# Scores and values of a sigmoid attention in one tile shape, with a routed block behind it

## The chip, the cores and the metric

The kernel runs on one core of a Trainium2 chip. The metric is the device time of one execution in microseconds.

## The reference

```python
# q, k, v: 8 x 12 x 448 x 64 (batch, head, token, width), float32
scores = scale * np.matmul(q, k.transpose(0, 1, 3, 2)) - np.log(S)
attn = 1.0 / (1.0 + np.exp(-scores))
attn_out = np.matmul(attn, v)
x = attn_out.transpose(0, 2, 1, 3).reshape(B, S, H * D)      # 8 x 448 x 768
scores = np.einsum('bsd,d->bs', x, w_gate)
out = x.copy()
for b in range(B):
    top_idx = np.argpartition(-scores[b], capacity)[:capacity]   # 128 of 448 tokens
    xe = x[b, top_idx]
    ye = np.maximum(xe @ w1, 0.0) @ w2                           # 768 -> 1024 -> 768
    g = 1.0 / (1.0 + np.exp(-scores[b, top_idx]))
    out[b, top_idx] = xe + g[:, None] * ye
```

## The kernel before, in words

The heads are taken four at a time (a quad: 32 of the 64 widths of four heads fill 128 partitions, `e` is the half of the width), and two quads make a stage `s`: there are twelve stages, and three quads a batch. `turn` transposes a quad's keys and queries on VectorE in blocks of 32. A stage has seven units (`unit`, L180): a unit makes the scores of 128 keys with 448 queries for four heads, in tiles of 32x128 (32 rows of the array for a head), two passes of `e`; unit 3 takes the last 64 keys of both quads instead, in tiles of 32x64. Its results fill two score tiles `psc` of two banks each, of a pool of three, and ScalarE turns each into a tile `attn` with one sigmoid over 896 columns (L200).

`values` (L204) multiplies attention by values one stage later: for each pair of heads `pr`, full pieces of 128 keys (L213, tile 128x64, two heads side by side) and half pieces of 64 keys (L224, 64x64), accumulated in the banks `oa` and `ob`, one for each quad of the stage. When a bank is complete, `take` (L235) transposes it into `x_b` on VectorE; `gate_part`, `gate` and `store` follow.

The routed block of a batch: `rank` (L268) spreads the gates over all partitions with a matmul by ones (L271), copies them (ScalarE, L274), transposes them, counts for each token how many are above it, in four places of 128 tokens (VectorE, L285 and L288), and makes the selection matrix `sel` (L295). `select` (L298) turns it into row numbers (L303) and gathers the rows `xe`. `turn_rows` (L317) transposes them on TensorE in two halves (L323), each copied to `xeT` by VectorE (L325). `ffn1` (L334; three groups, of 3, 3 and 2 blocks) and `ffn2` (L343; three groups) follow, and a scatter writes the rows.

All order is written out by hand in `stream`: after each unit come the value pieces that PACKED or SPREAD names for it, then short routed steps due there, then one group of the queue `ready` by `go`, mostly in bank `ob`. In the first two stages with values no routed group is ready. DMAs go in program order through SP's queue; `load_v(s)` is issued at the first unit of stage `s`, for use in stage `s + 1`. Every matmul of the program is recorded as two matmul instructions and two weight loads.

Of the kernel before, what the change touches and what calls it, by code (L numbers as in the profile page):

```python
# [9 lines left out]
F32 = mybir.dt.float32  # L10
# [7 lines left out]
def kernel(  # L18
# [48 lines left out]
    rows = ctx.enter_context(tc.tile_pool(name="rows", bufs=2))  # L67
    moe = ctx.enter_context(tc.tile_pool(name="moe", bufs=1))
    ps_sc = ctx.enter_context(tc.tile_pool(name="ps_sc", bufs=3, space=PSUM))
    ps_a = ctx.enter_context(tc.tile_pool(name="ps_a", bufs=1, space=PSUM))  # L70
    ps_b = ctx.enter_context(tc.tile_pool(name="ps_b", bufs=1, space=PSUM))

    def bank(which):
        if which == "psc":
            return ps_sc.tile([P, 2, 512], F32, name="psc")[:, 0]
        return (ps_a if which == "oa" else ps_b).tile([P, 512], F32, name=which)
# [52 lines left out]
    earlier = const.tile([P, NC, S], F32, name="earlier")  # L129
# [50 lines left out]
    def unit(s, n):  # L180

        psc = [ps_sc.tile([P, 2, 512], F32, name="psc") for _ in range(2)]
        if n == NF:
            parts = [(x, slice(HK, TB), x * Dh, Dh) for x in range(2)]
        else:
            x, c = divmod(n, NF + 1)
            parts = [(x, slice(4 * c, 4 * c + 4), 0, P)]
        for e in range(2):
            for x, blk, p0, np_ in parts:
                for h in range(4):  # L190
                    d = slice(h * TT, (h + 1) * TT)
                    nc.tensor.matmul(  # L192
                        psc[h // 2][p0:p0 + np_, h % 2, :S],
                        kT[2 * s + x][d, e, blk, :].rearrange("d r t -> d (r t)"),
                        qT[2 * s + x][d, e].rearrange("d r t -> d (r t)"),
                        start=(e == 0), stop=(e == 1))
        for pr in range(2):
            a = attnp.tile([P, 2, S], F32, name=f"attn{pr}", bufs=(NU + 1, NU + 3)[pr])
# [3 lines left out]
    x_tiles, gate_parts, st = {}, {}, {}  # L202

    def values(s, pr, what):  # L204

        tv, th = raw_v[s]
        if (s, pr) not in outs:
            outs[s, pr] = [bank("oa"), bank("ob")]
        o = outs[s, pr]
        if what[0] == "f":  # L210
            _, x, c = what
            for j in range(2):
                nc.tensor.matmul(  # L213
                    o[x][j * Dh:(j + 1) * Dh, :S],
                    tv[:, 4 * x + 2 * pr + j, c * Dh:(c + 1) * Dh],
                    attn[s, pr, (NF + 1) * x + c][:, j, :],
                    start=(x == 0 and c == 0), stop=(x == 1 and c == NF - 1))
            if (x, c) == (1, NF - 1):
                take(s, pr, 1)
        else:  # L220
            for x in range(2):
                p = slice(x * Dh, (x + 1) * Dh)
                for j in range(2):
                    nc.tensor.matmul(  # L224
                        o[x][j * Dh:(j + 1) * Dh, :S], th[p, 2 * pr + j, :],
                        attn[s, pr, NF][p, j, :], start=(x == 1), stop=(x == 0))
            take(s, pr, 0)

    def take(s, pr, x):

        b, g = divmod(2 * s + x, NG)
        if g == 0 and pr == 0:
            x_tiles[b] = rows.tile([P, TB, HP, TT], F32, name="x_b")
            gate_parts[b] = rows.tile([P, TB, NG], F32, name="gate_p")
        nc.vector.transpose(x_tiles[b][:, :, 2 * g + pr, :],  # L235
                            outs[s, pr][x][:, :S].rearrange("p (r t) -> p r t", t=TT))
# [31 lines left out]
    def rank(b, where="oa"):  # L268
        tg = tok_gate[b % 2]
        ps = bank(where)  # L270
        nc.tensor.matmul(ps[:, :S], ones, st[b].pop("diag").rearrange("p r t -> p (r t)"),  # L271
                         start=True, stop=True)
        rep = moe.tile([P, S], F32, name="rep")
        nc.scalar.activation(rep, ps[:, :S], AF.Copy)  # L274
        rep_t = moe.tile([P, TB, TT], F32, name="scr")
        nc.vector.transpose(rep_t, ps[:, :S].rearrange("p (r t) -> p r t", t=TT))
        for a in range(4):
            p = slice(a * TT, (a + 1) * TT)
            n = len(range(a, TB, 4))
            nc.vector.tensor_copy(tg[p, :n, 1], rep_t[p, a:TB:4, 0])  # L280
        for c in range(NC):
            n = P if c < NC - 1 else LAST
            own = tg[:n, c, 1:2]
            junk = moe.tile([P, S], F32, name="scr")
            nc.vector.tensor_scalar(out=junk[:n], in0=rep[:n], scalar1=own, scalar2=0.0,  # L285
                                    op0=ALU.is_gt, op1=ALU.add, accum_out=above[:n, c:c + 1])
            junk = moe.tile([P, S], F32, name="scr")
            nc.vector.scalar_tensor_tensor(  # L288
                out=junk[:n], in0=rep[:n], scalar=own, in1=earlier[:n, c, :],
                op0=ALU.is_equal, op1=ALU.mult, accum_out=level[:n, c:c + 1])  # L290
        place = moe.tile([P, NC], F32, name="place")
        nc.vector.tensor_add(place, above, level)
        for c in range(NC):
            n = P if c < NC - 1 else LAST
            nc.vector.tensor_scalar(out=sel[:n, c], in0=iota_r[:n], scalar1=place[:n, c:c + 1],  # L295
                                    scalar2=None, op0=ALU.is_equal)

    def select(b, s0, n, where):  # L298

        tg = tok_gate[b % 2]  # L300
        pk = bank(where)
# [15 lines left out]
    def turn_rows(b, n, half, where="oa"):  # L317
        if half == 0:
            st[b]["xeT"] = moe.tile([P, KD, P], F32, name="xeT")
        ps = bank(where).rearrange("p (k n) -> p k n", n=P)  # L320
        for t in range(3):
            tt = half * 3 + t
# [188 lines left out]
```

## Time and profile before

| | |
|---|---|
| median of 3 runs | 545.96 us (541.93 to 546.1) |
| the profiled execution | 545.69 us, span 543.9 us |
| TensorE busy | 500.3 us, 92% of the span |
| VectorE, ScalarE busy | 223.4 us, 177.5 us |
| mean granted TensorE clock | 0.97 |

The span runs from the first to the last recorded instruction; the rows are from this execution. PE is TensorE's matmul, PEld its weight loads, DVE VectorE, ACT ScalarE, POOL GpSimd, SP the engine that issues most DMAs. A record of PE that ends a block is shown until its modelled end, so the step from one block's start to the next one's tells more than its length.

### The profile page before, as it was taken

What the parts mean: (1) busy time and instruction counts of PE and PEld (TensorE: products, weight loads), DVE (VectorE), ACT (ScalarE), POOL (GpSimd) and SP (SyncE); (2) the same over time, 40 slices, a digit from 0 to 9 for tenths busy, and PEclk for the clock granted to TensorE, in tenths of its full rate; (3) what the DMA queues carried; (4) which work ended last, traced back from release to release, by engine and by line L of the source; (5) the groups of instructions that cost most, each with busy time, mean ns of one, the idle gap of its engine ahead of it and who ended that gap; (6) DMA issues with size and microseconds to landing.
All of it is one profiled execution on the core that took longest, in us unless ns stands there. A gap on an engine that the chain in (4) does not pass through costs nothing. (4 is left out here: it accounts for less than half of the span.)

```text
span 543.9 us, 8454 instructions
## 1 busy us (share of the span) xinstructions
PE 500.3 (92%) x3584; PEld 288.2 (53%) x3584; DVE 223.4 (41%) x474; ACT 177.5 (33%) x209; POOL 27.3 (5%) x46
## 2 busy tenths in 40 slices
PE   4999987989999999949999999995899999988995
PEld 2333333355565664526566566444357457558894
DVE  3307284573531482581062067177115216455101
ACT  3845451533332343232342343341334234101010
POOL 8000000000000000000000000000100000000100
PEclk9999997989999999998999999997999999999899
DMA  8694988989135379289124157758802007537200
GB/s 249 174 277 151 250 165 157 287 141 207 32 103 130 56 128 252 48 129 256 33 69 119 48 97 133 208 90 144 231 4 65 30 7 127 100 64 127 71 30 29
DMA packets 203397, 68.28 MB, mean 126 GB/s; under 512 B 182048, under 2 KB 194400, under 8 KB 203360
## 3 DMA queue, kind: packets, MB, share of 16 engines
q1 hardware_dynamic: 201952, 61.36, 52.0%
q0 software_dynamic: 1408, 6.39, 3.7%
q8 instruction: 28, 0.46, 0.4%
q14 instruction: 9, 0.07, 0.0%
HBM read 42.57 MB, written 25.17 MB: 125 GB/s over the span
## 5 line engine op out<-in xcount | busy, mean ns | idle before, releaser
L200 ACT ACTIVATE attn<-psc,bias_s 128x896 f32<-128x896 f32 x168 | 160.2, 1004 | 191.8 <-PE psc L192 185.8
L192 PE MATMUL psc<-qT,kT 32*128 32x448 f32 (+1 forms) x1536 | 157.8, 567 | 9.1 <-DVE qT L178 6.5
L192 PEld LDWEIGHTS psc<-qT,kT 32*128 32x128 f32 (+1 forms) x1536 | 63.7, 174 | 79.1 <-issue 53.6
L334 PE MATMUL ob<-xeT,w_sb 128*128 128x128 f32 x576 | 73.6, 289 | 13.2 <-DVE xeT L325 13.2
L334 PEld LDWEIGHTS ob<-xeT,w_sb 128*128 128x128 f32 x576 | 71.1, 203 | 22.3 <-DVE xeT L325 13.5
L213 PE MATMUL ob<-attn,raw_v 128*64 128x448 f32 x288 | 61.1, 552 | 0.0
L235 DVE STREAM_TRANSPOSE x_b<-oa 128x448 f32<-128x448 f32 x24 | 15.6, 650 | 108.6 <-PE oa L224 108.5
L213 PE MATMUL oa<-attn,raw_v 128*64 128x448 f32 x288 | 59.9, 548 | 0.0
L343 PE MATMUL ob<-w_sb,hT 128*128 128x256 f32 x256 | 58.9, 383 | 0.0
L343 PEld LDWEIGHTS ob<-w_sb,hT 128*128 128x128 f32 x256 | 47.3, 190 | 12.6 <-issue 6.8
L213 PEld LDWEIGHTS ob<-attn,raw_v 128*64 128x64 f32 x288 | 18.1, 137 | 41.3 <-issue 41.3
L213 PEld LDWEIGHTS oa<-attn,raw_v 128*64 128x64 f32 x288 | 18.5, 136 | 37.4 <-issue 35.8
L235 DVE STREAM_TRANSPOSE x_b<-ob 128x448 f32<-128x448 f32 x24 | 15.6, 650 | 50.3 <-PE ob L213 50.3
L175 DVE STREAM_TRANSPOSE kT<-raw_k 128x384 f32<-128x384 f32 x48 | 24.6, 549 | 16.3 <-PE psc L192 11.1
L336 ACT ACTIVATE hT<-ob 128x384 f32<-128x384 f32 (+1 forms) x18 | 8.2, 455 | 69.1 <-PE ob L334 57.0
L343 PE MATMUL psc<-w_sb,hT 128*128 128x256 f32 x128 | 30.2, 396 | 0.0
L343 PEld LDWEIGHTS psc<-w_sb,hT 128*128 128x128 f32 x128 | 25.2, 199 | 4.3 <-issue 0.7
L345 DVE SCALAR_TENSOR_TENSOR xe<-ob,gate,xe 128x256 f32<-128x256 f32 x16 | 7.7, 479 | 46.4 <-PE ob L343 46.4
L248 DVE TENSOR_REDUCE gate_p<-scr 128x14 f32<-128x896 f32 x24 | 26.1, 1087 | 0.8
L334 PE MATMUL psc<-xeT,w_sb 128*128 128x128 f32 x192 | 23.8, 288 | 2.6 <-DVE xeT L325 2.6
L224 PE MATMUL ob<-attn,raw_h 64*64 64x448 f32 x96 | 24.1, 579 | 2.1 <-ACT gate L310 2.1
L242 DVE TENSOR_TENSOR scr<-x_b,wg_b 128x896 f32<-128x896 f32 x24 | 25.7, 1070 | 0.3
(62 smaller groups left out, 257.7 us busy)
## 6 DMA issues: line engine op xcount, KB each, us to landing
raw_k<-in_k_dram SPq DMA_DIRECT2D x24, 448.0 KB
raw_q<-in_q_dram SPq DMA_DIRECT2D x24, 448.0 KB
x_d<-x_b SPq DMA_DIRECT2D x32, 336.0 KB
out_dram<-x_b SPq DMA_DIRECT2D x32, 336.0 KB
raw_v<-in_v_dram SPq DMA_DIRECT2D x48, 192.0 KB
w_sb<-in_moe_w_dram SPq DMA_DIRECT2D x6, 512.0 KB
w_sb<-in_moe_w_dram SPq DMA_DIRECT2D x8, 384.0 KB
raw_h<-in_v_dram SPq DMA_DIRECT2D x48, 32.0 KB
```

The source lines that it names most:

```text
L175: nc.vector.transpose(kT[i][:, e, :HK], sk[:, e, :HK].rearrange("p (m c) d -> p c m d", c=NF))
L192: nc.tensor.matmul(psc[h // 2][p0:p0 + np_, h % 2, :S], kT[2 * s + x][d, e, blk, :].rearrange("d r t -> d (r t)"), qT[2 * s + x][d, e].rea ...
L200: nc.scalar.activation(a, psc[pr][:, :, :S], AF.Sigmoid, bias=bias_s, scale=QK_SCALE)
L213: nc.tensor.matmul(o[x][j * Dh:(j + 1) * Dh, :S], tv[:, 4 * x + 2 * pr + j, c * Dh:(c + 1) * Dh], attn[s, pr, (NF + 1) * x + c][:, j, :], ...
L224: nc.tensor.matmul(o[x][j * Dh:(j + 1) * Dh, :S], th[p, 2 * pr + j, :], attn[s, pr, NF][p, j, :], start=(x == 1), stop=(x == 0))
L235: nc.vector.transpose(x_tiles[b][:, :, 2 * g + pr, :], outs[s, pr][x][:, :S].rearrange("p (r t) -> p r t", t=TT))
L242: nc.vector.tensor_tensor(out=tmp, in0=x_tiles[b][:, :, 2 * g:2 * g + 2, :].rearrange("p r h d -> p r (h d)"), in1=wg_b[:, 2 * g:2 * g + 2 ...
L248: nc.vector.tensor_reduce(out=gate_parts[b][:, :, g], in_=tmp, axis=AX.X, op=ALU.add)
L334: nc.tensor.matmul(ps[:, f - f0, :n], w1_sb[:, t, f * P:(f + 1) * P], xeT[:, t, :n], start=(t == 0), stop=(t == KD - 1))
L336: nc.scalar.activation(st[b]["hT"][:, f0:f1, :n], ps[:, :f1 - f0, :n], AF.Relu)
L343: nc.tensor.matmul(ps[:n, :ND], st[b]["hT"][:, t, :n], w2_sb[:, t, cols], start=(t == 0), stop=(t == KF - 1))
L345: nc.vector.scalar_tensor_tensor(out=xe[:n, cols], in0=ps[:n, :ND], scalar=st[b]["gate"][:n, 0:1], in1=xe[:n, cols], op0=ALU.mult, op1=ALU ...
```

## The change

Scores and values both use tiles of 32x64. A unit is split into two parts of 64 keys, side by side in the array. The values of a stage's four pairs (two quads, two pairs each) are made together in four rounds: in round `n` the row group `r` of the array works for pair `r ^ n`, so that in each round each of the four row groups writes to another bank, and after four rounds each pair has had all four. Round 0 comes after the last unit of the stage, rounds 1 to 3 after the first three units of the next; rounds 0 and 1 also take the 64 keys of unit 3. After each of the first three rounds ScalarE copies one element into a spare column of the bank written last.

The score pool has two tiles instead of three; the four other banks are two tiles `o0` and `o1`, which hold the values of the four pairs from round 0 until they are taken, are lent to the routed block between rounds 3 and 0 (in turn), and to units 1, 3 and 5 of stage 0. `select` uses a score tile. Routed groups stand after units 3, 4 and 5 (two after unit 5). `rank` becomes `spread`, four `rank` of one place each, and `place`, due at two points. `turn_rows` is done at once, with one copy on ScalarE. `earlier` has bytes instead of floats. The value load of the next stage is issued at the first unit of a stage, the second quad's turn after unit 1, the next stage's after unit 5.

The diff is cut to its core; lines that it removes are left out of it, they stand in the kernel above.

```diff
...
+    ps_sc = ctx.enter_context(tc.tile_pool(name="ps_sc", bufs=2, space=PSUM))
+    ps_o = [ctx.enter_context(tc.tile_pool(name=f"ps_o{n}", bufs=1, space=PSUM))
+            for n in range(2)]
+    turns = [0]
+    def banks(which):
         if which == "psc":
+            return ps_sc.tile([P, 2, 512], F32, name="psc")
+        if which == "o":
+            turns[0] ^= 1
+            which = turns[0]
+        return ps_o[which].tile([P, 2, 512], F32, name=f"o{which}")
...
+        if s == 0 and n in (1, 3, 5):
+            psc = [banks(0), banks(1)]
+        else:
+            psc = [banks("psc"), banks("psc")]
         if n == NF:
+            parts = [(x, HK) for x in range(2)]
         else:
             x, c = divmod(n, NF + 1)
+            parts = [(x, 4 * c), (x, 4 * c + 2)]
         for e in range(2):
+            for y, (x, r) in enumerate(parts):
                 for h in range(4):
                     d = slice(h * TT, (h + 1) * TT)
                     nc.tensor.matmul(
+                        psc[h // 2][y * Dh:(y + 1) * Dh, h % 2, :S],
+                        kT[2 * s + x][d, e, r:r + 2, :].rearrange("d r t -> d (r t)"),
                         qT[2 * s + x][d, e].rearrange("d r t -> d (r t)"),
                         start=(e == 0), stop=(e == 1))
         for pr in range(2):
+            a = attnp.tile([P, 2, S], F32, name=f"attn{pr}", bufs=NU + 3)
...
+    def values(s, n):
         tv, th = raw_v[s]
+        if n == 0:
+            outs[s] = [banks(0), banks(1)]
+        o = outs[s]
+        first = (0, 2, 2, 0)[n]
+        quads = [(first + m) % 4 for m in range(4)]
+        work = [(r, c) for c in range(NF) for r in quads]
+        if n < 2:
+            at = 4 * (NF - 1)
+            work[at:at] = [(r, None) for r in quads]
+        for r, c in work:
+            x, pr = divmod(r ^ n, 2)
+            rows = slice(r * TT, (r + 1) * TT)
             for j in range(2):
+                if c is None:
+                    w, a = th[rows, 2 * pr + j, :], attn[s, pr, NF]
+                else:
+                    w = tv[rows, 4 * x + 2 * pr + j, c * Dh:(c + 1) * Dh]
+                    a = attn[s, pr, (NF + 1) * x + c]
+                nc.tensor.matmul(o[x][j * Dh:(j + 1) * Dh, pr, :S], w, a[rows, j, :],
+                                 start=(n == 0 and c == 0), stop=(n == 3 and c == NF - 1))
+        if n < 3:
+            nc.scalar.activation(o[x][Dh:Dh + 1, pr, S:S + 1], bias_s[Dh:Dh + 1], AF.Copy)
         else:
             for x in range(2):
+                for pr in range(2):
+                    take(s, pr, x)
...
+    def spread(b, where="o"):
         tg = tok_gate[b % 2]
+        ps = banks(where)[:, 0, :S]
...
+        st[b]["rep"] = rep
+    def rank(b, c):
+        tg, rep = tok_gate[b % 2], st[b]["rep"]
+        n = P if c < NC - 1 else LAST
+        own = tg[:n, c, 1:2]
...
+    def place(b):
+        pl = moe.tile([P, NC], F32, name="place")
+        nc.vector.tensor_add(pl, above, level)
...
+    def turn_rows(b, n, where="o"):
+        xeT = moe.tile([P, 2, KD // 2, P], F32, name="xeT")
+        ps = banks(where).rearrange("p a (k n) -> p a k n", n=P)
+        for t in range(KD):
+            a, i = divmod(t, KD // 2)
+            nc.tensor.transpose(ps[:, a, i, :n], st[b]["xe"][:n, t * P:(t + 1) * P],
                                 iden[:n, :n])
+        nc.scalar.activation(xeT[:, :, :, :n], ps[:, :, :KD // 2, :n], AF.Copy)
+        st[b]["xeT"] = xeT.rearrange("p a k n -> p (a k) n")
...
+    def routed(b):
+        s = (NG * b + NG - 1) // 2 + 1
+        at = 5 if b == 0 else 4
+        put(late, s, at, spread, b)
+        for c in range(NC - 1):
+            put(late, s, at, rank, b, c)
+        put(late, s, 6, rank, b, NC - 1)
+        put(late, s, 6, place, b)
+        if s == NS:
+            return
+        for s0, n in SLOTS:
+            put(early, s + 1, 0, select, b, s0, n, "psc")
+            put(late, s + 1, 3, turn_rows, b, n)
+            put(late, s + 1, 3, routed_groups, b, n)
+    def gates(i):
+        gate_part(i)
+        b, g = divmod(i, NG)
+        if g == NG - 1:
+            store(b)
+            gate(b)
+    def gap(s, n):
+        due(early, s, n)
+        if n < 3 and s > 0:
+            values(s - 1, n + 1)
+            if n == 2:
+                gates(2 * s - 2)
+        if 3 <= n < NU - 1:
+            if not ready:
+                due(late, s, n)
+            go()
+            if n == NU - 2 and s < NS - 2:
+                go()
+        if n == NU - 1 and s < NS:
+            values(s, 0)
+        due(late, s, n)
+        if n == 3 and s > 0:
+            gates(2 * s - 1)
     def stream():
+        for b in range(B):
+            routed(b)
...
+                if n == (0 if s == 0 else 1):
                     turn(2 * s + 1)
                     load(2 * s + 3)
+                if n == 0:
+                    load_v(s + 1)
                     load_weights(5 * s - 5, 5 * s)
...
+                gap(s, n)
+                if n == NU - 2:
                     turn(2 * s + 2)
                     load(2 * s + 4)
...
+        for n in range(5):
+            gap(NS, n)
+        for n in range(3):
+            go()
+        due(late, NS, NU - 1)
         for s0, n in SLOTS:
+            select(B - 1, s0, n)
         while ready:
+            go()
         for s0, n in SLOTS:
+            turn_rows(B - 1, n)
+            routed_groups(B - 1, n)
         while ready:
+            go()
+        assert not early and not late
...
```

## Rows read from the trace of the kernel before

**Rows 1.** Timeline of PE, 424 to 470 us: start, length, line, tiles, records

```profile
424.04 2.48 PE L213 MATMUL oa<-attn,raw_v 128*64 128x448 f32 x12
426.45 3.72 PE L343 MATMUL ob<-w_sb,hT 128*128 128x256 f32 x16
430.10 1.79 PE L192 MATMUL psc<-qT,kT 32*128 32x448 f32 x16
431.81 0.59 PE L224 MATMUL oa<-attn,raw_h 64*64 64x448 f32 x2
...
432.73 2.48 PE L213 MATMUL ob<-attn,raw_v 128*64 128x448 f32 x12
...
439.25 4.29 PE L334 MATMUL ob<-xeT,w_sb 128*128 128x128 f32 x36
443.47 1.76 PE L192 MATMUL psc<-qT,kT 32*64 32x448 f32 x32
...
467.52 1.05 PE L303 MATMUL psc<-tok_gate,sel 128*128 128x2 f32 x8
468.50 0.59 PE L224 MATMUL oa<-attn,raw_h 64*64 64x448 f32 x2
```

**Rows 2.** Timeline of PE's weight loads around unit 3 of a stage

```profile
219.37 0.23 PEld L192 LDWEIGHTS psc<-qT,kT 32*64 32x64 f32 x16 [0.33 <-issue]
219.80 0.18 PEld L192 LDWEIGHTS psc<-qT,kT 32*64 32x64 f32 x8 [0.20 <-issue]
220.18 0.18 PEld L192 LDWEIGHTS psc<-qT,kT 32*64 32x64 f32 x8 [0.20 <-issue]
221.06 0.14 PEld L224 LDWEIGHTS oa<-attn,raw_h 64*64 64x64 f32 x2 [0.70 <-issue]
```

**Rows 3.** Timeline of PE, two value pieces in a row

```profile
34.78 0.97 PE L213 MATMUL ob<-attn,raw_v 128*64 128x448 f32 x4
35.59 1.67 PE L213 MATMUL oa<-attn,raw_v 128*64 128x448 f32 x8
37.19 1.34 PE L192 MATMUL psc<-qT,kT 32*64 32x448 f32 x18
```

**Rows 4.** Waits of PE: us in total, times, longest

```profile
PE ob L334 <- DVE xeT L325: 13.2, 2, 6.6
...
PE ob L303 <- DVE sel L295: 4.5, 1, 4.5
...
PE psc L334 <- DVE xeT L325: 2.6, 2, 2.2
```

**Rows 5.** The six stretches at low clock: busy us, granted clock, DMA share

```profile
85.00:91.80 6.80, 6.80 (x33) 2.97 (x34) 2.90 (x8) 2.08 (x3) 1.11 (x1) 0.50 0.84 148
...
sum 30.10, PE 24.92 PEld 19.62 DVE 13.05 ACT 2.62 POOL 2.10; mean PE 4.15 PEld 3.27 DVE 2.17 ACT 0.44 POOL 0.35
```

**Rows 6.** Timeline of ScalarE in stage 0

```profile
14.24 1.91 ACT L200 ACTIVATE attn<-psc,bias_s 128x896 f32<-128x896 f32 x2 [0.26 <-PE psc L192]
17.13 1.91 ACT L200 ACTIVATE attn<-psc,bias_s 128x896 f32<-128x896 f32 x2 [0.98 <-PE psc L192]
```

**Rows 7.** Timeline of VectorE during a ranking

```profile
234.71 0.65 DVE L276 STREAM_TRANSPOSE scr<-oa 128x448 f32<-128x448 f32 x1 [1.36 <-ACT rep L274]
...
236.11 0.68 DVE L285 TENSOR_SCALAR_CACHE_REDUCE scr<-rep,tok_gate 128x448 f32<-128x448 f32 x1
...
241.89 0.16 DVE L292 TENSOR_TENSOR place<-above,level 128x4 f32<-128x4 f32 x1
...
242.88 0.54 DVE L325 COPY xeT<-oa 128x384 f32<-128x384 f32 x1
```

**Rows 8.** Stage 3 and the tail: busy us, granted clock, DMA share, GB/s

```profile
77.70:120.90 43.20, 36.22 (x248) 17.17 (x245) 25.39 (x63) 14.55 (x17) 1.11 (x1) 0.88 0.93 193
...
465.10:538.40 73.30, 68.97 (x415) 55.38 (x414) 23.27 (x59) 3.62 (x9) 3.92 (x4) 0.95 0.35 68
```

**Rows 9.** Groups by line: busy us, mean ns of one

```profile
L274 ACT ACTIVATE rep<-oa 128x448 f32<-128x448 f32 x7 | 3.8, 544 | 4.0 <-PE oa L271 4.0
```

More of the change, by code (lines that the diff above doesn't have):

```diff
@@ L280, in rank, with select @@
             nc.vector.tensor_copy(tg[p, :n, 1], rep_t[p, a:TB:4, 0])
+        st[b]["rep"] = rep
[3 more added lines that the diff above has]
+        own = tg[:n, c, 1:2]
+        junk = moe.tile([P, S], F32, name="scr")
+        nc.vector.tensor_scalar(out=junk[:n], in0=rep[:n], scalar1=own, scalar2=0.0,
+                                op0=ALU.is_gt, op1=ALU.add, accum_out=above[:n, c:c + 1])
+        junk = moe.tile([P, S], F32, name="scr")
+        nc.vector.scalar_tensor_tensor(
+            out=junk[:n], in0=rep[:n], scalar=own, in1=earlier[:n, c, :],
+            op0=ALU.is_equal, op1=ALU.mult, accum_out=level[:n, c:c + 1])
+    def place(b):
+        pl = moe.tile([P, NC], F32, name="place")
+        nc.vector.tensor_add(pl, above, level)
         for c in range(NC):
             n = P if c < NC - 1 else LAST
[L283 to L295, printed above, removed]
+            nc.vector.tensor_scalar(out=sel[:n, c], in0=iota_r[:n], scalar1=pl[:n, c:c + 1],
                                     scalar2=None, op0=ALU.is_equal)
-    def select(b, s0, n, where):
+    def select(b, s0, n, where="o"):
         tg = tok_gate[b % 2]
-        pk = bank(where)
+        pk = banks(where)[:, 0]
         for c in range(NC):
@@ L315, in select @@
         st[b].update(idx=idx, gate=gt, xe=xe)
[L317 to L322, printed above, removed]
-            nc.tensor.transpose(ps[:, t, :n], st[b]["xe"][:n, tt * P:(tt + 1) * P],
+    def turn_rows(b, n, where="o"):
[4 more added lines that the diff above has]
+            nc.tensor.transpose(ps[:, a, i, :n], st[b]["xe"][:n, t * P:(t + 1) * P],
                                 iden[:n, :n])
-        nc.vector.tensor_copy(st[b]["xeT"][:, half * 3:half * 3 + 3, :n], ps[:, :3, :n])
+        nc.scalar.activation(xeT[:, :, :, :n], ps[:, :, :KD // 2, :n], AF.Copy)
+        st[b]["xeT"] = xeT.rearrange("p a k n -> p (a k) n")
     def ffn1(b, n, f0, f1, where):
@@ L330, in ffn1 @@
             st[b]["hT"] = moe.tile([P, KF, P], F32, name="hT")
-        ps = bank(where).rearrange("p (k n) -> p k n", n=P)
+        ps = banks(where)[:, 0].rearrange("p (k n) -> p k n", n=P)
         for f in range(f0, f1):
@@ L338, in ffn2 @@
     def ffn2(b, n, part, where):
-        ps = bank(where)
+        ps = banks(where)[:, 0]
         xe = st[b]["xe"]
@@ L361, in routed_groups, with go @@
             ready.append((ffn2, (b, n, part)))
-    def go(where="ob"):
+    def go(where="o"):
         if ready:
@@ L402, in pieces, with put, due @@
-    def pieces(s, plan, n):
-        for pr, ps in plan.get(n, []):
-            for w in ps:
-                values(s, pr, w)
+    early, late = {}, {}
+    def put(where, s, n, fn, *args):
+        where.setdefault((s, n), []).append((fn, args))
+    def due(where, s, n):
+        for fn, args in where.pop((s, n), []):
+            fn(*args)
+    def routed(b):
[12 more added lines that the diff above has]
+            put(late, s + 1, 3, routed_groups, b, n)
```

132 lines of the change are left out of this document (12 added, 120 removed).

## The prediction

> **What bounds the kernel now.** The page comes first: TensorE (PE) is busy for 500.3 of 543.9 us, VectorE for 41%, ScalarE for 33% of the span, so the time is PE's order of work, and what counts is what PE does in it and where it stands. The timeline of PE alone then tells what one block of work costs, from its start to the next block's start [rows 1]: a full value piece (12 matmul records, tile 128x64) 2.41, a half piece (8 records, 64x64) 0.92, a unit of scores (16 records, 32x128) 1.71, a group of ffn1 4.22 with 36 records (so 2.8 with 24), a group of ffn2 3.65, a selection 0.98.
>
> How much of that is work? The weight loads inside the middle unit, the one that runs in 32x64 already, follow each other every 0.38 us [rows 2]: one pass of 448 columns, during which eight tiles run side by side. Its four passes are 1.50 us, and the unit takes 1.69: 0.19 goes at its ends. By the same count an ordinary unit loses 0.21, a full piece (six passes, 2.25) 0.16, a half piece (two passes, 0.75) 0.17. The spreading of a gate, two such passes and an end, I put at 0.85. Two value pieces of one shape that follow each other, four records and eight, take 0.81 and 1.60 us [rows 3]: 2.41 for six passes, with two banks and two sets of waits, as if they were one piece. So what is lost at an end belongs to the change of shape, as far as these rows tell, not to a new bank or a new wait.
>
> The rest is waiting and clock. PE waits for xeT twice 6.6 us and, in the tail, once 2.2, and 4.5 us for the first selection [rows 4]. During or behind each of these the granted clock is 1.2 instead of 2.4 GHz for a while: the stretch at 85 us is the one behind the 4.5, and there are six, 30.1 us in all, which cost some 15 us [rows 5].
>
> **Shapes, part by part.** Before there are 84 units, 48 full and 24 half pieces: 84 x 0.21 + 48 x 0.16 + 24 x 0.17 = 29 us at their ends. The passes stay the same: a stage has 7 units of 4 passes, and its values are 4 x 6 + 2 x 2 = 28 passes before, (4 + 4 + 3 + 3) x 2 = 28 after; all 56 are 21.0 us. After, scores and values have one shape, and only a routed block breaks it: three or four stretches of 32x64 in a stage with routed work, one in the first three, some 37 in all, times 0.19 = 7 us. That is 22 us less.
>
> **Two score tiles instead of three.** A unit now takes both tiles of the pool, so it can't end before ScalarE has emptied both. A pair of sigmoids takes 1.91 us [rows 6]; I estimate 2.2 us from the end of a unit's stream to its second tile being free: 0.2 until its last record has ended (the records of a unit end 1.79 us after its start, and 1.50 is stream [rows 1]), 1.91, and 0.1 for the two hand-overs. A value round of three groups lasts 2.25, one of four 3.0: both just cover it. If that cover is short by 0.2 us, it costs 0.2 for two units in each of eleven stages, 4 us. Where no routed work is ready, in stages 1 and 2, the units 3 to 6 stand back to back. The middle unit of stage 0 had that case: its sigmoid came 2.89 us after the one before, instead of 2.16 [rows 6], so about 1.6 us after the tile came free. A blocked unit then costs 2.2 + 1.6 = 3.8 instead of 1.5; three of them make 6.8 us a stage. In stage 0 the units alternate with the lent output banks, and ScalarE sets the pace (about 1.95 a unit); the first value round falls in its last microseconds. I get the end of the first unit of stage 1 at 26.0 us, where it is 26.4 now, with 3.0 us of values already done.
>
> **The selection takes a score tile** right after a unit, and waits for the first sigmoid: 0.9 us in stages 4, 6, 7, 9 and 10. In stage 3 it waits for `sel`: the gate is spread after the sixth unit of stage 2, then VectorE has 1.4 of transposing and copies and four places in 5.8 us, 1.44 each [rows 7], and the turn of the next heads between the third and the fourth, which I estimate at 2.4 us (1,792 columns where a transpose of 448 takes 0.65). I get 4.5 us of waiting, as today, with the low clock behind it.
>
> **turn_rows on ScalarE.** Today its second copy queues on VectorE behind a whole ranking: the copy at 242.88 starts when the places and their selection are done [rows 7], and that is the first of the two waits of 6.6 us. After, there is one copy of 768 columns on ScalarE, estimated at 0.87 us from 0.54 for 448 [rows 9] and 0.95 for 896, half a pair [rows 6]. Where nothing is ready (stages 3, 6, 9), transposes, copy and ffn1 follow directly on unit 3, and the copy queues behind its two sigmoids: PE waits 2.2 us. Such a wait of 2.2 was followed by a low clock before, so I add 1.7 us (half of 3.4) in stages 6 and 9, and 3.4 in stage 3.
>
> **Lent output banks.** The first routed group of a stage needs a bank whose two takes have run, transposes of 448 columns, 0.65 us each [rows 7]. Counting the alternation by hand, it gets the first bank, free in time, but in stages 5 and 8 the second: 1.1 us each.
>
> **Costed at nothing.** The small ScalarE copy at a round's end runs during the next unit (1.5 us) or group; uncovered it costs 0.4, as between the last rounds of the tail, where I count 0.8. The ranks divided over places run beside ffn groups; the byte-wide `earlier` is read where a four-byte one took half a place's 1.44 us, and if bytes were twice as slow, 2.8 us would be added where ranks are waited for (stage 3, tail). `load_v` of the next stage now waits at the head of SP's queue until the third round is over, with weights, the second load and the store behind it. In stages 1 to 3 that idles a queue that moves some 200 GB/s today [rows 8]. At 0.21 MB a us I get the load that stage 2 turns at its second unit landed some 2 us before it is needed, and the last of w2 5 us before; nothing is lost, but 10 us would be if the cover went.
>
> **The sum,** from first value piece to first value piece. Every stage has 21.0. By the order of the queue of routed groups, stages 3, 6 and 9 have three groups of ffn1 and one of ffn2 (4.2 + 4.2 + 2.8 + 3.55, a group behind another saving some 0.1 of its end), 4 and 7 two and two, 5 and 8 one (the short one) and three, 10 one and two, 11 two and one. Stages 1 and 2: + 6.8, 27.8 and 27.9. Stage 3: + selection 1.0 and 4.5 + four stretch ends 0.8 + turn 0.85 and 2.2 + ffn 14.75 + spread 0.85 + clock 3.4 = 49.4. Stages 4 and 7: + 1.0 + 0.9 + 0.8 + 0.75 + ffn 15.6 = 40.0. Stages 5 and 8: + 0.6 + 1.1 + ffn 13.6 + 0.85 = 37.1. Stages 6 and 9: + 1.9 + 0.8 + 3.05 + 14.75 + 0.85 + 1.7 = 44.0. Stage 10: + 1.9 + 0.8 + 0.75 + 11.5 = 35.9. Stage 11: - 1.5 (no unit follows) + 0.6 + 10.6 + 0.85 = 31.6. From 26.0 that leads to 440.8 us. The last three rounds with their selection: 9.5. The tail has 1.2 of waiting for a bank, two ffn2 groups (7.2), a turn (0.75), a spread (0.85), ffn1 and a selection (11.8), ffn2 (10.5), a turn with 1.1 of waiting (1.85), and ffn1 and ffn2 of the last batch (21.3): 55.4. Its ranks, some 8 us after the last round plus 9, are covered by 11 us of ffn1. PE ends at 505.7; today it ends at 538.4 (the last stretch of [rows 8]), 5.5 before the span does, so the span is 511.2. The profiled execution took 545.69 for a span of 543.9: 513.0 us, 32.7 below it. The median of 545.96 is the same execution time for this purpose. The gain is 22 of shapes, about 3 of stage 0, about 8 of clock; the waits come out even (31 before, 34 after).
>
> **A rival on the other side: PE is fed too slowly.** A pass in 32x64 has sixteen instructions (eight loads, eight matmuls), where an ordinary unit had eight and a full piece four. It holds 0.375 us only if one leaves every 23 ns. For it: the one block of 32x64 in a stage has just 64 of them, and its neighbours are no denser than 53 ns each (32 in a unit's 1.71 us, 72 in the 4.22 of ffn1 [rows 1]); a run of 512 is not shown. Against it: those 64 go at 26 ns on average, ends included, and the first sixteen loads in 0.23 us [rows 2]. It decides from 26 ns, where 16 x 2.9 ns x 672 passes eat up the 32 us; at 30 ns a pass is 0.48 and the kernel takes 513 + 70 = 583. The Trainium skill (TensorE: Matmul & The Clock Gate, "Wait — 56ns, not 53.3ns?") says that without decoding in hardware a matmul costs the sequencer about 62 ns; eight of them would make a pass of 0.50 us, and the kernel about 84 us slower than my sum, an estimate from that page. The 64 above don't agree with it, unless they were queued beforehand.
>
> **Ends that stay.** If each unit and round pays its end whatever the shape, as a price of its waits, 95 more ends of 0.19 come back: 513 + 18 = 531. For it: all ends in the trace but those in rows 3 go with a change of shape. Against it: rows 3.
>
> **Covers that go.** Late loads in stages 2 and 3 (10), units after short rounds (4), a low clock in the thinly filled stages 1 and 2 (3): 523 to 530. For it: DMA is busy for 0.93 of stage 3 [rows 8]; against it: two of the three need a cover to be some 10% shorter than I reckon it.
>
> **How the numbers follow.** The forecast, 500 to 523: 0.60. Covers that go, 523 to 530: 0.10. Ends that stay, 528 to 536: 0.13. Faster than 500 (no wait after turns, no low clock): 0.05. Nothing measurable, 540 to 551: 0.04, or slower, mostly by the feeding of PE: 0.08. A measurement of this kernel can tell about 1% from no change, so faster is 0.87, same 0.05, slower 0.08. The range runs from 500 to 536.
>
> **What the profile after would show.** In the timeline, the loads of units and rounds every 0.375 us across their borders, and 12 us from unit 0 to unit 3 of a stage; blocked units of 3.8 us in stages 1 and 2; the waits for xeT at three stages and 2.2 us; a wait for `sel` of 4 to 5 us at about 82 us; fewer stretches at half clock. Wrong would be: passes of 0.45 us in long stretches, gaps of 0.2 between unit and round, waits for raw_k or raw_q after 50 us.

## The result, and the profile after

The changed kernel takes 524.57 us (median of 4 runs, 521.8 to 528.43) where the kernel before, on the same chip, takes 546.03 (541.93 to 547.15): a ratio of 0.963, 95% interval [0.956, 0.970]. On a second chip it was 526.69 (6 runs), ratio 0.962 [0.957, 0.967]. The forecast of 513.0 had the sign, and the stated range of 500 to 536 holds the time, but the gain is 21 us and not 33; the median lies outside the 500 to 523 of the forecast itself, in the band that went to "Covers that go". The profiled execution took 521.8 for a span of 520.0, so against the forecast span of 511.2 there are 8.8 us to explain; the median lies another 2.8 above this execution.

On the page PE is busy for 476.0 of 520.0 us, the 92% of before. A share can't show what happened; the timeline of PE across the end of stage 4 does, as [rows 1] did before:

```profile
168.61 1.76 PE L202 MATMUL psc<-qT,kT 32*64 32x448 f32 x32
170.16 1.71 PE L237 MATMUL o<-attn,raw_v 32*64 32x448 f32 x32
171.66 0.96 PE L237 MATMUL o<-attn,raw_h 32*64 32x448 f32 x16
172.42 0.96 PE L237 MATMUL o<-attn,raw_v 32*64 32x448 f32 x16
173.17 1.71 PE L202 MATMUL psc<-qT,kT 32*64 32x448 f32 x32
174.67 1.71 PE L237 MATMUL o<-attn,raw_v 32*64 32x448 f32 x32
```

Take starts, not lengths. A unit goes from 173.17 to 174.67, 1.50 us, where it was 1.71 [rows 1]; a round of four groups from 170.16 to 173.17, 3.01 for eight passes. The 0.2 at each end (the time lost where a block gives way to one of another shape) is gone, from unit to round and from round to unit. Where the waits are now:

```profile
PE psc L202 <- DVE qT L184: 10.2, 2, 6.5
PE o L357 <- ACT xeT L347: 6.7, 4, 1.9
PE psc L202 <- ACT attn L210: 5.8, 6, 1.1
PE o L366 <- ACT gate L333: 4.5, 1, 4.5
PE psc L326 <- ACT attn L210: 4.5, 4, 1.1
PE psc L326 <- issue: 2.3, 2, 1.2
PE o L357 <- DVE x_b L252: 2.2, 2, 1.1
PE o L366 <- DVE x_b L252: 1.5, 1, 1.5
PE o L237 <- ACT o L240: 0.8, 2, 0.4
```

The two waits of 6.6 us for xeT [rows 4] have become waits of 1.9, a little less than costed. Two rows were in no term of my sum: 3.7 of the first one (the other 6.5 is the start of the kernel, as before), and 4.5 us for a gate. Without the start they add up to 32 us; I had 34. But the two are not counted alike: my 34 has the blocked units of stages 1 and 2 by their starts, 6.8 us a stage, where these rows have only the idle time ahead of their records, 5.8 in all.

```profile
40.26 2.65 PE L202 MATMUL psc<-qT,kT 32*64 32x448 f32 x32 [1.14 <-ACT attn L210]
44.02 2.65 PE L202 MATMUL psc<-qT,kT 32*64 32x448 f32 x32 [1.11 <-ACT attn L210]
```

By its starts (PE, stage 1) a blocked unit takes 3.76, and from unit 3 of a stage to round 0 it is 12.55 us in stages 1 and 2, 6.5 above the four units' 6.0. Counted as I counted, the waits are some 39 us. Set against the forecast, the start of round 1 (from the prediction's stage lengths, with the selection ahead of the round):

| | forecast | measured | behind |
|---|---|---|---|
| stage 1 | 26.0 | 26.4 | 0.4 |
| stage 2 | 53.8 | 54.2 | 0.4 |
| stage 3 | 87.2 | 91.2 | 4.0 |
| stage 6 | 210.1 | 214.1 | 4.0 |
| stage 7 | 254.1 | 256.5 | 2.4 |
| stage 10 | 375.2 | 376.2 | 1.0 |
| end of the last round | 450.3 | 452.0 | 1.7 |
| end of PE | 505.7 | 514.5 | 8.8 |

So the misses stand in two places, ahead of stage 3 and in the tail, and some 3 us come back in between. Ahead of stage 3, PE first:

```profile
84.94 3.29 PE L202 MATMUL psc<-qT,kT 32*64 32x448 f32 x32 [3.66 <-DVE qT L184]
89.40 1.84 PE L326 MATMUL psc<-tok_gate,sel 128*128 128x2 f32 x8 [1.16 <-issue]
91.17 3.29 PE L237 MATMUL o<-attn,raw_v 32*64 32x448 f32 x32
```

and VectorE in the same microseconds:

```profile
78.33 0.68 DVE L306 TENSOR_SCALAR_CACHE_REDUCE scr<-rep,tok_gate 128x448 f32<-128x448 f32 x1
...
82.57 1.03 DVE L181 STREAM_TRANSPOSE kT<-raw_k 128x384 f32<-128x384 f32 x2
...
83.72 1.07 DVE L184 STREAM_TRANSPOSE qT<-raw_q 128x896 f32<-128x896 f32 x1
84.71 0.63 DVE L306 TENSOR_SCALAR_CACHE_REDUCE scr<-rep,tok_gate 64x448 f32<-64x448 f32 x1
```

I had this order right, the turn of the next heads between the third place and the fourth. What I didn't ask is who waits for that turn: unit 0 of stage 3, which stands ahead of the selection. It waits 3.66 us for qT behind three places of 1.4 us; the selection then waits 1.16 instead of 4.5. And the clock, in the view of stretches (busy us, granted clock, DMA share):

```profile
84.20:94.40 10.20, 8.30 (x80) 4.08 (x88) 5.22 (x16) 2.08 (x3) 1.11 (x1) 0.50 0.79 128
108.10:111.50 3.40, 3.40 (x18) 3.40 (x18) 3.02 (x5) 0.00 (x0) 0.00 (x0) 0.50 1.14 279
480.20:487.00 6.80, 5.11 (x12) 4.12 (x13) 0.56 (x2) 0.17 (x1) 0.97 (x1) 0.50 0.29 95
451.95:514.53 62.58, 55.58 (x342) 49.85 (x342) 18.65 (x45) 5.07 (x10) 2.94 (x3) 0.95 0.33 64
```

At half clock PE loses half of its busy time: 4.2 and 1.7 us in stage 3, where I had 3.4. The last row is the tail, 62.6 us instead of 55.4. There the timelines of PE, of VectorE and of GpSimd show one knot:

```profile
481.89 9.67 PE L366 MATMUL o<-w_sb,hT 128*128 128x256 f32 x32 [4.54 <-ACT gate L333]
```

```profile
481.42 0.16 DVE L331 TENSOR_SCALAR idx<-o 128x1 int32<-128x1 f32 x1 [7.43 <-DMA out_dram<-xe,idx]
```

```profile
478.35 0.99 POOL L372 DMA_INDIRECT out_dram<-xe,idx  x1 [33.95 <-DMA out_dram<-x_b]
```

Read from the bottom: the scatter of batch 5 starts at 478.35, when the last store to the output (that of batch 7, ahead of it in program order) has landed. The row numbers `idx` of batch 7 take the tile that this scatter reads, and wait 7.43 us on VectorE. The gate's sigmoid, which empties the output bank that the selection was lent, runs behind `idx`; the second group of ffn2 needs that bank, waits 4.5 us and begins at half clock.

### The profile page after: what moved, and what is told of

Its sections match the earlier page's. It is cut to its first block, busy times and chain, and to the rows that moved or that the text cites. A ratio compares the mean times of both kernels' runs of the same rounds, so it can differ in the third digit from the quotient of the medians.

```text
span 520.0 us, 14605 instructions
## 1 busy us (share of the span) xinstructions
PE 476.0 (92%) x6656; PEld 304.6 (59%) x6656; DVE 210.9 (41%) x458; ACT 189.8 (36%) x253; POOL 27.3 (5%) x46
## 5 line engine op out<-in xcount | busy, mean ns | idle before, releaser
L202 PE MATMUL psc<-qT,kT 32*64 32x448 f32 x2592 | 155.0, 551 | 16.0 <-DVE qT L184 10.2
L237 PE MATMUL o<-attn,raw_v 32*64 32x448 f32 x2304 | 132.8, 542 | 0.8 <-ACT o L240 0.8
L202 PEld LDWEIGHTS psc<-qT,kT 32*64 32x64 f32 x2592 | 60.0, 133 | 83.8 <-issue 50.1
L357 PEld LDWEIGHTS o<-xeT,w_sb 128*128 128x128 f32 x768 | 88.7, 195 | 19.6 <-issue 7.8
L357 PE MATMUL o<-xeT,w_sb 128*128 128x128 f32 x768 | 92.1, 280 | 8.9 <-ACT xeT L347 6.7
L366 PE MATMUL o<-w_sb,hT 128*128 128x256 f32 x384 | 89.9, 391 | 6.0 <-ACT gate L333 4.5
L366 PEld LDWEIGHTS o<-w_sb,hT 128*128 128x128 f32 x384 | 73.2, 195 | 24.8 <-issue 6.6
L237 PEld LDWEIGHTS o<-attn,raw_v 32*64 32x64 f32 x2304 | 57.0, 133 | 51.0 <-issue 43.3
L252 DVE STREAM_TRANSPOSE x_b<-o 128x448 f32<-128x448 f32 x48 | 26.9, 617 | 124.4 <-PE o L237 98.8
L237 PE MATMUL o<-attn,raw_h 32*64 32x448 f32 x384 | 26.1, 537 | 0.0
```

Source lines behind the costliest of these rows:

```text
L202: nc.tensor.matmul(psc[h // 2][y * Dh:(y + 1) * Dh, h % 2, :S], kT[2 * s + x][d, e, r:r + 2, :].rearrange("d r t -> d (r t)"), qT[2 * s + ...
L237: nc.tensor.matmul(o[x][j * Dh:(j + 1) * Dh, pr, :S], w, a[rows, j, :], start=(n == 0 and c == 0), stop=(n == 3 and c == NF - 1))
L252: nc.vector.transpose(x_tiles[b][:, :, 2 * g + pr, :], outs[s][x][:, pr, :S].rearrange("p (r t) -> p r t", t=TT))
L357: nc.tensor.matmul(ps[:, f - f0, :n], w1_sb[:, t, f * P:(f + 1) * P], xeT[:, t, :n], start=(t == 0), stop=(t == KD - 1))
L366: nc.tensor.matmul(ps[:n, :ND], st[b]["hT"][:, t, :n], w2_sb[:, t, cols], start=(t == 0), stop=(t == KF - 1))
```

## The experiments

The theory: what the change removes are the ends at changes of shape, some 0.2 us each, and what it lost against the forecast are two waits with the low clock behind them. Rivals: the gain comes from something else in the change (the wait for xeT, stage 0); an end is the price of a block, whatever its shape; and each wait only covers the next one. Each run has its ratio to the kernel before on its own chip.

**The 72 ordinary units back to 32x128**, all else as after (the third element of `parts` is the first row of the tile, the fourth the number of blocks):

```diff
-            parts = [(x, 4 * c), (x, 4 * c + 2)]
+            parts = [(x, 4 * c, 0, 4)]
-            for y, (x, r) in enumerate(parts):
+            for x, r, p0, nb in parts:
```

> The changed kernel, only the 72 ordinary units of scores back in tiles of 32x128; same passes, same banks, same order and waits. If the ends belong to the change of shape, a stage with routed work has about ten blocks with an end of 0.16 to 0.21 us instead of three or four: some 1.2 us in each of nine stages and about 1 in stages 1 and 2, together 11 to 16 us slower than the changed kernel, 535 to 541 us, and gaps of about 0.2 us between a unit and the round behind it. If the ends are the price of each block's waits and banks, they are already gone or stay whatever the shape: within 3 us of the changed kernel, 521 to 528.

Measured: 536.32 us, ratio 0.986 [0.979, 0.992], 11.8 more than after. Timeline of PE in stage 4:

```profile
137.01 1.79 PE L202 MATMUL psc<-qT,kT 32*128 32x448 f32 x16
138.72 2.51 PE L237 MATMUL o<-attn,raw_v 32*64 32x448 f32 x48
141.16 1.78 PE L202 MATMUL psc<-qT,kT 32*128 32x448 f32 x16
```

The unit is 1.71 again, and the round behind it, whose own code is that of after, 2.44 instead of the 2.26 it took between units of its own shape. So the end belongs to the change of shape, and a block of another shape brings two of them, one as it begins and one as it ends. In stages 4, 5, 7 and 8, where neither profile has low clock, a stage is 1.2 to 1.4 us longer than after, as expected. The edit does one thing more, where units stand back to back (stage 1):

```profile
43.50 2.67 PE L202 MATMUL psc<-qT,kT 32*128 32x448 f32 x16 [0.39 <-ACT attn L210]
46.56 2.67 PE L202 MATMUL psc<-qT,kT 32*128 32x448 f32 x16 [0.39 <-ACT attn L210]
```

A blocked unit comes every 3.06 us instead of 3.76, so that stage 1 is as long as after (27.9 and 27.8). The 11.8 us are what is left of the ends after this, and still over half of the gain.

**The other way round: units in two parts of 64 keys in the kernel before,** where the values keep their shapes.

```diff
-            parts = [(x, slice(4 * c, 4 * c + 4), 0, P)]
+            parts = [(x, slice(4 * c + 2 * y, 4 * c + 2 * y + 2), y * Dh, Dh) for y in range(2)]
```

> The kernel before, only its ordinary units split into two parts of 64 keys, so that all scores are in tiles of 32x64; the values stay in 128x64 and 64x64. If the ends belong to the change of shape, nothing is gained, since each unit still has other shapes on both sides: a unit 1.69 instead of 1.71 us, 0 to 2 us in all, 543 to 546. If sixteen instructions a pass cost by themselves (a slower feed), it is slower by more than 4 us; if the split itself were the gain, it is faster by more than 8.

Measured: 554.95 us, ratio 1.014 [1.008, 1.021]. I had expected no change, and it is 9 us slower. Where units have values as neighbours they take 1.69 us (204.97 to 206.66), so one shape alone gains nothing, as the theory says. The loss is elsewhere, first in stage 0:

```profile
16.69 1.87 PE L192 MATMUL psc<-qT,kT 32*64 32x448 f32 x32 [0.99 <-ACT attn L200]
19.57 1.87 PE L192 MATMUL psc<-qT,kT 32*64 32x448 f32 x32 [1.02 <-ACT attn L200]
...
29.84 2.48 PE L213 MATMUL oa<-attn,raw_v 128*64 128x448 f32 x12
```

Units back to back on the pool of three tiles come every 2.87 us instead of 2.16 (both by their starts), and the first value piece starts at 29.84 instead of 26.38. Up to the end of PE the granted clock was low for 44.4 us of this profile, 30.7 in that of before; at most half of the difference, 7 us, is time (4 by half of PE's busy time in these stretches). The middle unit of stage 0 had already shown the longer step [rows 6], and it is the same 0.7 us with three score tiles (2.87 and 2.16) as with two (3.76 and 3.06). The order of the matmuls offers a cause: in the narrow unit the second part's heads 0 and 1 stand in program order behind the first part's heads 2 and 3, which need the second score tile, so the first tile is complete only near the unit's end. From the end of PE's wait to the next sigmoid it is 1.83 us here (16.69 to 18.52) and 1.10 in the kernel before (18.19 to 19.29), a difference of about two passes. That cause is argued, not shown: no run has the heads outside the parts.

**The copy of turn_rows on ScalarE, alone in the kernel before:**

```diff
-        nc.vector.tensor_copy(st[b]["xeT"][:, half * 3:half * 3 + 3, :n], ps[:, :3, :n])
+        nc.scalar.activation(st[b]["xeT"][:, half * 3:half * 3 + 3, :n], ps[:, :3, :n], AF.Copy)
```

> The kernel before, only the copies of turn_rows moved from VectorE to ScalarE. If the two waits of 6.6 us for xeT and their low clock come from the ranking in VectorE's queue, these waits shrink to about 2 us (the copy behind two sigmoids), and 9 us of waiting and 3 to 7 us of low clock go: 530 to 534 us. If the wait is only exchanged for one on ScalarE's queue, nothing measurable: 541 to 549.

Measured: 549.88 us (10 runs), ratio 1.007 [1.004, 1.010]. The two waits of 6.6 us went, and PE waits 21.0 us in two others, soon after (timelines of PE and of VectorE):

```profile
258.38 1.75 PE L224 MATMUL ob<-attn,raw_h 64*64 64x448 f32 x4 [10.69 <-ACT gate L310]
```

```profile
257.90 0.16 DVE L308 TENSOR_SCALAR idx<-ob 128x1 int32<-128x1 f32 x1 [12.63 <-DMA out_dram<-xe,idx]
```

It is the knot of the tail, in the kernel before: `idx` waits for the scatter of an earlier batch, which GpSimd starts at 249.40. The wait for xeT had covered it: without the edit the scatter starts at 249.19 and `idx` at 257.39, after a wait of 2.44, so PE comes to the same half pieces (L224) at nearly the same time, 257.87 and 258.38. With the new waits stand two stretches of 13.7 us at half clock. So this part of the change is worth nothing by itself; the two waits go only in the new order of the whole.

**Three tiles for `idx`,** in the kernel after (`bufs=2` to `bufs=3`).

> The changed kernel, only the tile idx with three buffers instead of two. In the tail the row numbers of the last batch wait 7.4 us for the scatter of two batches before, which waits for the last store; PE waits 4.5 us behind it and then runs 6.8 us at half clock. If the buffer is what ties them, both go: 5 to 8 us faster than the changed kernel, 517 to 520. If the gather behind the same scatter in GpSimd's queue is what counts, PE waits as long for xe one step later: within 2 us of the changed kernel, 522 to 527.

Measured: 522.82 us, ratio 0.960 [0.954, 0.966], not to be told from after. The wait for the gate went and 2.3 us for the gathered rows came, GpSimd:

```profile
483.43 0.99 POOL L372 DMA_INDIRECT out_dram<-xe,idx  x1 [34.39 <-DMA out_dram<-x_b]
487.20 0.97 POOL L335 DMA_INDIRECT xe<-x_d,row  x1 [2.79 <-issue]
```

The scatter still stands until the last store has landed, and now the gather queues behind it. Half of the wait is gone, and from the end of the last round to the end of PE it is 59.1 us instead of 62.6; but this profile has stretches at half clock in stages 6 and 9, where the first profile of after has none.

**A second routed group between units of the tail,** one block earlier, so that the queue is shorter at its end.

```diff
-            if n == NU - 2 and s < NS - 2:
+            if (n == NU - 2 and s < NS - 2) or (n == 3 and s == NS):
```

> The changed kernel, only the last ffn2 group of the sixth batch, and so its scatter, ahead of the last store in program order. If the scatter waits for that store, and the row numbers, the gate and the gather of the last batch for the scatter, all of it goes: no wait of 4.5 us, no low clock at 480 us, 6 to 9 us faster than the changed kernel, 515 to 519. If the buffer of the row numbers alone is the knot, no more than with three buffers for them: 521 to 524.

Measured: 522.26 us, ratio 0.951 [0.944, 0.959] (another chip, on which before takes 550.16). Much less than the 6 to 9 us that I expected if the scatter was all of it: the tail is 60.7 us instead of 62.6, since the wait for the gate is exchanged for one for `sel`. The last place of the ranking now stands on VectorE behind the group that was moved, and ends too late:

```profile
480.77 1.02 PE L326 MATMUL o<-tok_gate,sel 128*128 128x2 f32 x8 [2.50 <-DVE sel L318]
```

**The first gate spread one unit earlier** (`at = 5 if b == 0 else 4` to `at = 4`).

> The changed kernel, only the spreading and first three rankings of the first batch due after unit 4 of stage 2 instead of unit 5. In the changed kernel the turn of the next heads stands on VectorE behind these rankings, unit 0 of stage 3 waits 3.7 us for qT, and 10.2 us of low clock follow. If the order on VectorE is the cause, the wait goes, the selection waits only the 1.1 us for its score tile, and the low clock at about 84 us goes or halves: stage 3 starts 5 to 8 us earlier, 517 to 520 us. If the load of the heads is what is late, the wait stays: 522 to 527.

Measured: 518.22 us, ratio 0.944 [0.937, 0.952]. The 3.7 us for qT are gone, and of the 13.6 us at half clock in stage 3 there are 3.4 left. From round 1 of stage 1 to that of stage 3 it is 58.7 us instead of 64.8: a wait of 3.7 us was worth 6, because the clock came back with it.

**The selection behind round 1 instead of ahead of it** (`put(early, ...)` to `put(late, ...)`).

> The changed kernel, only the selection placed behind the value round that follows unit 0 instead of ahead of it. If its wait of 1.1 us (six times) is for the score tile that ScalarE still reads, it goes, and unit 1 waits some 0.6 us for the selection's own readers instead: 2 to 4 us faster, 520 to 522. If unit 1 then pays as much as the selection did, within 1 us of the changed kernel.

Measured: 516.06 us, ratio 0.939 [0.932, 0.946]. Timeline of PE in stage 4:

```profile
135.22 1.05 PE L326 MATMUL psc<-tok_gate,sel 128*128 128x2 f32 x8
```

The selection no longer waits, since the round has given ScalarE its time. It is more than I expected, but this chip had no run of after beside it, so the size waits for the combination below.

**Unit 4 of stages 1 and 2 in the lent output banks,** as three units of stage 0 have it:

```diff
-        if s == 0 and n in (1, 3, 5):
+        if (s == 0 and n in (1, 3, 5)) or (s in (1, 2) and n == 4):
```

> The changed kernel, only unit 4 of stages 1 and 2 in the lent output banks. If two score tiles are what makes the blocked units 3.8 us, the three of them take 8.7 us instead of 11.3 in each of the two stages (then ScalarE's pace): 4 to 6 us faster up to the start of stage 3, part of which is lost there, since the rankings of the first batch end no earlier by as much: 519 to 523 us. If the pace of ScalarE rules already, nothing.

Measured: 520.24 us (515.58 to 523.53), ratio 0.942 [0.932, 0.951]. Timeline of PE in stage 1:

```profile
38.42 2.34 PE L202 MATMUL o<-qT,kT 32*64 32x448 f32 x26
...
44.05 3.19 PE L202 MATMUL psc<-qT,kT 32*64 32x448 f32 x26 [1.40 <-ACT attn L210]
```

One blocked unit less in each of the two stages, and from round 1 of stage 1 to that of stage 3 it is 59.6 us instead of 64.8; but this profile has nine stretches of 3.4 us at half clock, four of them in stages 6 and 9, behind the waits of 1.1 and 1.9 us that after has there too. What the edit gained ahead of stage 3 was lost again behind it in this execution; the shortest of the four, 515.58, shows that it need not be.

**The repairs together, and after again beside them on one chip.** First `at = 4`, the late selection and three `idx`; then unit 4 of stage 1 in the lent banks too.

> The changed kernel once more, unchanged, as the measure for the two beside it. If the 522 to 525 us of the first chip are the kernel's own, it gives 519 to 528 here. If the second chip, where two small repairs gave 516 and 518 us, is simply quicker with the new order of work, it gives 515 to 519.

> The changed kernel with three of its waits taken away together: the first gate spread one unit earlier (the 3.7 us before the first unit of stage 3), every selection behind the round instead of before it (five waits of 1.1 us and the one of 1.2), three tiles for the scatter's row numbers (part of the 4.5 us in the tail). If the waits are added up on PE's path, it is 4 + 5 + 2 = 11 us below the changed kernel, less up to 3 that other waits take over: 510 to 517 us. If each wait taken away only uncovers the next one (as the copy on ScalarE and the early tail group did), it stays within 4 us of the better of the two repairs: 514 to 519 us, no more than 6 below the changed kernel.

> As the one before, with unit 4 of stage 1 in the lent output banks too, so that one of the three blocked units of stage 1 has free banks. By the row of the stages with that edit, some 2.5 us of PE's wait go in stage 1: 2 to 3 us below the one before. If the idle time was only moved, or comes back as low clock, as it did when both stages lent their banks, it is the same within 1.5 us.

Measured: 526.69, 509.57 and 504.53 us (6 runs each), ratios 0.962 [0.957, 0.967], 0.932 [0.927, 0.936] and 0.924 [0.919, 0.929]. The three repairs are worth 17 us where I added up 11, and the fourth another 5. In the profile of the three PE waits for qT at the start alone, and of the waits for the gate and its gather one is left:

```profile
PE o L345 <- DMA xe<-x_d,row: 2.3, 1, 2.3
```

The rest is clock: up to the end of PE it is low for 27.3 us in the profile of after on this chip, for 6.8 with three repairs, for 3.4 with four. At most half of these 20.5 us is time, which covers the step from 11 to 17 with a few us to spare: a late selection saves some 0.6 us and not its wait of 1.1 (stage 4 is 1.7 us longer, stage 5 2.3 shorter than after). The fourth repair takes 3.1 us from stage 1, where I had some 2.5, and 1.9 from stage 3, where the stretch of 3.4 at half clock is gone. The rival, that each wait only uncovers the next, holds for single edits in the tail and not for these.

**The output stored first, the copy for the gather second,** on top of the four:

```diff
-        for dst in (x_d, out[b]):
+        for dst in (out[b], x_d):
```

> As the one before (all four repairs), with the rows of a batch stored to the output first and to the copy that the gather reads second. If the last wait of the tail is the scatter of batch 5 standing on GpSimd until the last store to the output has landed, the scatter goes some 10 us earlier (at 452 to 455 us instead of 464), the gather of batch 7 follows its row numbers at about 463, the wait of 2.5 us for xe goes and the low clock of 3.4 us behind it too: 2.5 to 4 us below the 504.5, 500 to 502 us. If the gather itself then waits for the copy, which lands some 8 us later than it did, the wait stays about as long: 503 to 506.

Measured: 515.5 us, ratio 0.945 [0.942, 0.948], 11 more than without it: neither theory. Timeline of PE, then GpSimd:

```profile
105.81 1.51 PE L345 MATMUL o<-iden,xe 128*128 128x128 f32 x6 [12.79 <-DMA xe<-x_d,row]
```

```profile
97.89 1.11 POOL L335 DMA_INDIRECT xe<-x_d,row  x1 [85.05 <-DVE scr L259]
```

I had looked at the tail alone. In stage 3 the first gather goes at 97.89 instead of 86.48, since the copy now lands behind 13 us of stores, in a stage where DMA is busy for 0.93 of the time before [rows 8]: PE waits 12.8 us, with 13.7 at half clock. The gather's row names a step of VectorE that ended just before; the copy's last store, issued at 90.4, lands some 7 us later, at about 97. In the tail the edit did what it was for: no wait, no low clock, and from the end of the last round to the end of PE 55.3 us, where it was 59.5 with the four repairs and 62.6 after. My sum for the tail was 55.4. The edit for the later batches alone wasn't tried.

## Why the prediction was right, and where it was not

**The number.** That the range holds 524.57 is partly luck: it lies in the band of "Covers that go", 523 to 530 with a chance of 0.10, and none of its three covers went. After the start PE waits for no load, no unit but the blocked ones waits for a score tile, and no low clock comes before 84.2 us. What took the time, the turn of the heads behind a ranking and the scatter behind a store, stood in no rival.

**Ends at changes of shape, 22 us: right.** Units and rounds follow each other without an end, and undoing it for 72 units costs 11.8 us. From round 1 to round 1, stages 4, 5, 7, 8 and 10 take 37.9, 39.5, 37.9, 39.5 and 33.9 us, where the sum has 38.1, 39.0, 38.1, 39.0 and 34.0. Stage 0 gave its 3 us: round 1 begins at 26.36, with round 0 done, where the first value piece began at 26.38 before. "Ends that stay" fell with the first timeline. The Trainium skill (TensorEngine Tiling (Array Packing), "Key Properties") says that changing the tiling mode drains TensorE; the trace agrees, with 0.21 us for a unit and 0.18 for a round next to another shape.

**PE fed too slowly: refuted.** 32 matmuls and 32 loads leave in 1.50 us, 47 ns for a pair, over whole rounds and units. The 62 ns that the Trainium skill (TensorE: Matmul & The Clock Gate, "Wait — 56ns, not 53.3ns?") gives for a matmul without decoding in hardware aren't the rate of this execution; no run shows which way it decodes.

**The waits, 34 us: some 39 by the same count, two of them in other places.** The 32 of the rows only looks like my 34, since it leaves out most of what the blocked units lose; of the 5 us more, 4.5 are the gate's. Rows against rows the waits do come out even, 31 before and 32 after; the prediction set the rows of before beside a count by starts. Blocked units come every 3.76 us where I had 3.8, the wait for xeT is 1.9 where I had 2.2, the bank 1.1 as costed, the selection 1.1 where I had 0.9. The covers held: in no stage does PE wait for a load of keys, queries or values after the start.

**Stage 3, mis-sized.** The step that failed is "the selection takes a score tile ... In stage 3 it waits for `sel`": 4.5 us. The waits there are 3.66 for qT and 1.16, hardly more together. But they leave unit 0, selection and round 1 at half clock; the 3.4 us for the clock became 5.9. Moving the spread by one unit took the wait for qT and 10.2 of the 13.6 us at half clock away. For the turn I had 2.4 us, though its 1,792 columns at 0.65 for 448 make 2.6; it took 2.2 (82.57 to 84.79).

**The tail, mis-sized: 62.6 for 55.4.** The sum of its blocks was right, as the last experiment shows. What was missing is the knot of `idx`, scatter and last store: 4.5 us of wait and 2.6 lost at half clock (of 5.1 busy). I had counted what PE issues and VectorE computes there, and not what GpSimd's queue stands behind. The kernel before shows its traces too, as the wait for a gate at L224; the prediction left it out.

**Costed at nothing: held.** The small copies of ScalarE cost 0.8 in all, as counted, and the step of the ranking that reads the byte-wide `earlier` takes 683 ns on average, where it took 682 with floats.

**Clock, 8 us of gain: nearer to 4 in the first profile.** By half of PE's busy time in them, the low stretches up to PE's end cost 12.5 us before (24.92 in the sum of [rows 5]) and 8.4 after; I had 15 and 6.8. In stages 6 and 9 the low clock that I had added didn't come in this execution, which gave 3.4 us back; in the profile on the second chip one came at 230.1 us, right behind the wait for xeT in stage 6, and one at 380.3 in stage 10. That is much of why one profile has a span of 520.0 and the other 525.7.

What stays open: whether the order of heads and parts is why a blocked unit of 32x64 waits longer, and whether lending in stage 2 pays once its gate is spread early.

## What to carry to other kernels

Where blocks of two tile shapes alternate, count the changes and price each by how much longer a block takes, from start to start, than between others of its own shape; one shape on one side alone gains nothing. When a step is moved on a helper engine, ask of everything queued behind it who waits, and follow an indirect scatter back to the stores ahead of it in program order. And a wait on PE is worth more than its length when a low clock follows it: here waits of some 11 us brought 17 when they went together, while single waits, removed at the end of a chain, only uncovered the next.

## What the runs showed of the hardware that wasn't expected

The granted clock differs between executions of one kernel: the six of after on the second chip have means of 0.972 to 0.981 and 523.2 to 527.4 us, those with three repairs 0.990 to 0.996 and 507.6 to 510.9. It falls behind short waits too, and not behind each of them. This is the same group in stage 6, first in the profile of after on the first chip, then on the second:

```profile
229.19 4.29 PE L357 MATMUL o<-xeT,w_sb 128*128 128x128 f32 x36 [1.90 <-ACT xeT L347]
```

```profile
229.78 5.91 PE L357 MATMUL o<-xeT,w_sb 128*128 128x128 f32 x36 [1.76 <-ACT xeT L347]
...
378.34 1.05 PE L326 MATMUL psc<-tok_gate,sel 128*128 128x2 f32 x8 [1.13 <-ACT attn L210]
```

The first runs at 2.4 GHz, the second partly at 1.2, behind the shorter wait; and 1.9 us after the selection of the last row, which waited 1.13, another such stretch begins, at 380.3 us. The prediction counted low clocks behind waits of 2.2 us and more [rows 4, 5], but the kernel before already had two behind shorter ones. Its stretches at 112.3 and 504.9 us follow these:

```profile
111.58 0.55 PE L323 MATMUL oa<-iden,xe 128*128 128x128 f32 x3 [1.82 <-DVE xeT L325]
...
502.82 1.02 PE L303 MATMUL psc<-tok_gate,sel 128*128 128x2 f32 x8 [1.73 <-DVE sel L295]
```

The profiles with three and four repairs, where no selection waits, have no such stretch in stages 4 to 11; those with the late selection alone and with the output stored first, in which no selection waits either, still have one each, at 226.2 and 347.5, each within 0.6 us of the end of a wait of 1.9 for xeT.
